# Sliding-window attention with ALiBi feeding an ELU feed-forward: bias by matmul for one more unit, and the first chunks' schedule rearranged

## The chip, the cores and the metric

The kernel runs on one core of a Trainium2 chip. The metric is the device time of one execution in microseconds; the number that counts is the median of several executions. A core has five engines with a queue each: TensorE (PE; its weight loads are listed apart as PEld), VectorE (DVE), ScalarE (ACT), GpSimd (POOL) and SyncE (SP). Each engine takes its instructions strictly in the order in which the program issues them, and waits for the other engines through semaphores.

## The reference

Two parts. Attention with 8 batches, 8 heads, 576 positions and 64 dimensions a head; a position sees itself and the 127 before it, with a linear distance penalty by head (ALiBi). Its output, 4608 tokens by 512, goes through a feed-forward of 2048 hidden units with ELU.

```python
scores = q @ k.T / sqrt(64) - slope[head] * |i - j|      # kept where 0 <= i - j < 128
attn = softmax(scores)
x = (attn @ v).reshape(4608, 512)
h = x @ w_in
g = where(h > 0, h, exp(min(h, 0)) - 1)
out = g @ w_out
```

## The kernel before

The work is cut into *steps*, numbered from 0. A step is a group of hidden matmuls (`hidden`, L279: 16 matmuls of 128 columns, or the same amount otherwise cut) into one of the PSUM banks of `BUF`, followed by its exponential on ScalarE (L284), its minimum with 1 on GpSimd (L285) and, one step later, the last part of the ELU on VectorE (`elu`, L292; `done(s)` issues the elus of step s). TensorE may write the next group into a bank only when the elu of the group before it there has run. A dictionary `HID` gives each step its group, `OUT` its four output matmuls of 512 columns (L298), and `at(s, f, ...)`, `before`, `after` hang further work on a step. All is written out by hand: the order of issue is the order of these lists. In steps 18 to 23 there is no hidden group.

The attention is cut by batch b and *unit* u, a block of 128 keys with the 256 queries that see it; the fourth unit (u = 3) is 192 queries of key block 3 and 64 of the last, half-filled block 4. A unit is scores (L172 for batches 0 and 1, L221 for the others), exponentials into the tile EX (L201, L206, L227), and values with the sums beside them (`values`, L244), divided on VectorE (L250, L251) into xn. xn is then turned into xT, the layout in which the hidden groups read it: by four TensorE transposes and a copy (`turn` with a copy, L263 and L264) for the first two batches, by a DMA transpose on SP (L259) for later ones.

The distance penalty enters in one of two ways. For units 0 to 2 of batch 0 it is added ahead of the scores in PSUM by a matmul of a scaled identity SI with the table RB (`bias`, L161; `early_bias`, L179). For all others the exponential is multiplied on VectorE by a table TAB of exponentials (`first_weigh`, L212, for batches 0 and 1; `weigh`, L232, for the others). TAB has two halves, the second for u = 3, copied on VectorE at the start (L367, L368).

q and k of batches 0 and 1 are turned by TensorE (`turn_first`, L133, with copies in L137). From batch 2 on, q and k lie in a staging tile st, and VectorE transposes them in blocks (`turn_qk`, L141): eight instructions a batch, four for k and four for q, each over all 576 positions. `TURN` lists the steps of these eight for batch 2; for later batches they come two by two, every fourth step. `START[b]` is the first step of batch b from batch 2 on.

Loads (`load_first`, `load_qk`, `load_v`, `load_wi`, `load_wo`) are issued from GpSimd's queue and stand there between the minimums of L285. Stores and DMA transposes stand in SP's queue.

The steps around the change, in batch 0: the scores of the third unit in step 3, those of the fourth unit in steps 4 and 6, its multiplications in steps 6 and 8, its values in step 9, the turn of the third tile in step 6:

```python
        at(6, first_scores, 0, 3, 1, 0)
        at(6, turn, 0, 2, nc.scalar.copy, sp[3])
        at(6, first_weigh, 0, 3, 0)
        at(7, first_expo, 0, 3, 1, 0, 0, 256)
        at(8, first_weigh, 0, 3, 1)
        at(9, values, 0, 3, 0)
```

Of the kernel before, what the change touches and what calls it, by code (L numbers as in the profile page):

```python
# [8 lines left out]
F16 = mybir.dt.float16  # L9
I32 = mybir.dt.int32  # L10
AF = mybir.ActivationFunctionType
ALU = mybir.AluOpType
# [6 lines left out]
def kernel(  # L19
# [9 lines left out]
    nc = tc.nc  # L29
# [7 lines left out]
    R = S // 64  # L37
    V = nc.vector
# [10 lines left out]
    def one(shape, dt, name):  # L49
        return const.tile(shape, dt, name=name, tag=name)  # L50

    ident = one([128, 128], F16, "ident")

    RB = one([128, 256], F16, "RB")

    SI = one([128, H, 128], F16, "SI")

    TAB = one([128, 2, 4, 2, 256], F16, "TAB")
# [15 lines left out]
    sp = [spa[:, 0, :], spa[:, 1, :]] + [ps_s.tile([128, 512], F32, name=f"sp{i}", tag=f"sp{i}") for i in (2, 3)]  # L74
# [4 lines left out]
    pairs = [AB, sp[2:4], hp, [sp[3], op]]  # L79
# [44 lines left out]
    def turn_first(b, w, part, half, bank, copy):  # L124

        p0, n, m, r0, j0 = split(b, w, part)
        nh = 4 if n == 32 or m == 1 else 2
        t = bank.bitcast(F16)[:, 0:nh * m * n].rearrange("p (x j r) -> p x j r", x=nh, j=m)
        r = slice(p0, p0 + n)
        for x in range(nh):  # L130
            for j in range(m):
                for hh in range(2):
                    nc.tensor.transpose(t[64 * hh:64 * hh + 64, x, j, :], s0[b][r, w, 4 * hh + nh * half + x, j0 + j, :],  # L133
                                        ident[r, r])
        t = t.rearrange("p x j r -> p x r j")
        o = (Q0, K0)[w][b][:, nh * half:nh * half + nh, r0:r0 + m * n]
        copy(o.rearrange("p x (r j) -> p x r j", j=m), t)  # L137
# [7 lines left out]
    with tc.manual_schedule():  # L145
# [8 lines left out]
        def blocks(u):  # L154
            return [(0, u, 128 * u, 256)] if u < 3 else [(0, 3, 384, 192), (192, 4, 512, 64)]

        def bias(half, d):
            for x in (2 * half, 2 * half + 1):
                for hh in range(2):
                    c = 256 * (x % 2)  # L160
                    nc.tensor.matmul(pairs[d][hh][:, c:c + 256], SI[:, 4 * hh + x, :], RB,  # L161
                                     start=x % 2 == 0, stop=False, skip_group_check=True)

        def first_scores(b, u, half, d):

            heads = [(x, hh) for x in (2 * half, 2 * half + 1) for hh in range(2)]
            added = b == 0 and u < 3
            for o, kb, q0, n in blocks(u):
                for x, hh in heads:
                    r, c = slice(64 * hh, 64 * hh + 64), 256 * (x % 2) + o  # L170
                    k0 = x * S + 128 * kb
                    nc.tensor.matmul(pairs[d][hh][:, c:c + n], kt_[b][r, k0:k0 + 128], Q0[b][r, x, q0:q0 + n],  # L172
                                     start=not added, stop=True, skip_group_check=True)

        def early_bias(banks, c0):

# [147 lines left out]
        rel = one([128, 256], I32, "rel")  # L324
        far = one([128, 256], F16, "far")
# [24 lines left out]
        V.tensor_scalar(out=ident, in0=rel[:, 0:128], scalar1=0.0, scalar2=None, op0=ALU.is_equal)  # L350
        V.scalar_tensor_tensor(out=far, in0=rel, scalar=127.0, in1=rel, op0=ALU.subtract, op1=ALU.mult)
        V.tensor_scalar(out=far, in0=far, scalar1=0.0, scalar2=-BIG, op0=ALU.is_gt, op1=ALU.mult)
        V.scalar_tensor_tensor(out=RB, in0=rel, scalar=-1.0, in1=far, op0=ALU.mult, op1=ALU.add)
        slope = [2.0 ** (-8.0 * (h + 1) / H) for h in range(H)]
        for h in range(H):
            V.tensor_scalar(out=SI[:, h, :], in0=ident, scalar1=8.0 * slope[h], scalar2=None, op0=ALU.mult)
        V.memset(VP[0][:, :, :, D:D + 1], 1.0)

        for h in range(H):
            nc.scalar.activation(TAB[:, 0, h // 2, h % 2, :], RB, AF.Exp, scale=slope[h])  # L360
        warm(22)
        turn_first(0, 1, 0, 0, hp[0], V.tensor_copy)
        turn_first(0, 1, 0, 1, op, V.tensor_copy)
        early_bias(AB, 0)
        turn_first(0, 0, 0, 0, hp[1], nc.scalar.copy)
        turn_first(0, 0, 0, 1, av, V.tensor_copy)
        V.tensor_copy(TAB[:, 1, :, :, 0:192], TAB[:, 0, :, :, 0:192])  # L367
        V.tensor_copy(TAB[:, 1, :, :, 192:256], TAB[:, 0, :, :, 0:64])  # L368
        early_bias(sp[2:4], 128)
# [59 lines left out]
        at(3, turn_first, 0, 1, 1, 1, sp[3], nc.scalar.copy)  # L429
        at(3, turn_first, 0, 0, 2, 0, hp[1], nc.scalar.copy)  # L430
        for half in range(2):
            at(3, bias, half, 3 * half)
        for half in range(2):
            at(3, first_scores, 0, 2, half, 3 * half)
            at(3, first_expo, 0, 2, half, 3 * half, 0, 256)
        at(4, first_scores, 0, 3, 0, 0)
        at(4, first_expo, 0, 3, 0, 0, 0, 256)
        at(5, values, 0, 2, 0)
        at(5, values, 0, 2, 1, op)
        at(6, first_scores, 0, 3, 1, 0)  # L440
        at(6, turn, 0, 2, nc.scalar.copy, sp[3])
        at(6, first_weigh, 0, 3, 0)
        at(7, first_expo, 0, 3, 1, 0, 0, 256)
        at(8, first_weigh, 0, 3, 1)
        at(9, values, 0, 3, 0)
        at(9, values, 0, 3, 1, sp[3])
        at(10, values, 0, 4, 0)
# [4 lines left out]

        for n in range(4):
            at(n + 1, load_wo, n)
        at(4, load_first, 1, 1, 0)
        at(5, load_first, 1, 0, 0)
        at(8, load_first, 1, 1, 1)
        at(10, load_first, 1, 0, 1)
        for n, s in enumerate((6, 7, 11, 12, 13)):
            at(s, load_v, 1, n)  # L460
        at(16, turn_first, 1, 1, 0, 0, av, V.tensor_copy)
        at(16, turn_first, 1, 1, 0, 1, sp[3], nc.scalar.copy)
# [14 lines left out]


        START = [None, None, 32, 49, 66, 83, 100, 117]
        TURN = 20, 22, 23, 24, 24, 25, 27, 29  # L480
        for b in range(2, B):
            for u in range(4):
                a = START[b] + 4 * u
                after(a, scores, b, u)
                for g in range(4):
                    before(a + 1 + g // 2, expo, b, u, g)
                at(a + 1, weigh, b, u, 0)
                at(a + 2, weigh, b, u, 1)
                at(a + 3, values, b, u, 0, sp[2])
                at(a + 3, values, b, u, 1, sp[3])  # L490
                at(a + 3, turn, b, u)
                if u == 3:
                    at(a + 4, values, b, 4, 0, sp[0])
                    at(a + 4, values, b, 4, 1, sp[2])
                    at(a + 4, turn, b, 4)
            a = START[b - 1] if b > 2 else 0
            for n in range(8):
                at(a + 4 * (n // 2) if a else TURN[n], turn_qk, b, int(n < 4), *divmod(n % 4, 2))
                at(a - 8 + n if a else 14 + n // 2, load_qk, b, int(n < 4), n % 4)
            for n in range(5):  # L500
                at(a + 3 + n if a else 18 + n // 2, load_v, b, n)

        slots = set(HID) | set(OUT) | set(tasks) | set(early)
        for s in range(min(slots), max(slots) + 1):
            for f, a in early.get(s, []):
                f(*a)
            for step in HID.get(s, []):
                hidden(*step)
            if s > 1 and s - 1 in HID:
                done(s - 1)  # L510
            for f, a in tasks.get(s, []):
                f(*a)
# [34 lines left out]
```

## Time and profile before

| what | value |
|---|---|
| median of 8 runs | 322.5 us (321.99 to 323.92) |
| the profiled execution by its own time | 322.0 us |
| its span, first to last instruction | 320.2 us |
| TensorE busy | 311.7 us, 97% |
| VectorE busy | 218.8 us, 68% |
| ScalarE busy | 181.1 us, 57% |
| GpSimd busy | 169.2 us, 53% |
| TensorE clock granted | full, in all slices of the page |

The profile is of one execution. Times in it are microseconds from the start of the span. A timeline row gives start, duration, engine, line and operation, the tiles written and read, the shape, the count of like instructions merged, and in brackets how long the engine was idle before it and what ended that. A waits row gives who waited for whom, total, number of times and the longest. Matmuls overlap their neighbours, and their ends are modelled; what TensorE takes is best read from one start to the next.

### The profile page before, as it was taken

Reading aid. Unit: us, or ns where it says so; the run is one execution under the profiler, and the core shown is the slowest. Engines: PE = TensorE matmul, PEld = TensorE weight load, DVE = VectorE, ACT = ScalarE, POOL = GpSimd, SP = SyncE. Lnnn points to the kernel's source line nnn. Section 1 sums busy time; section 2 is a strip of 40 time slices with the busy share of each in tenths; the row PEclk is TensorE's granted clock in tenths of the full one; section 3 lists DMA queues with packets and bytes.
Section 4 is the critical chain, followed back from the end, with each engine's and each line's share of the span. In section 5 each row is a group of like instructions: output and inputs, shape, how many; then the busy total and the mean of one; then the engine's idle time right before and its main releaser. Section 6 shows DMA issues by size and latency. Waiting matters only on the chain.

```text
span 320.2 us, 9418 instructions
## 1 busy us (share of the span) xinstructions
PE 311.7 (97%) x3967; PEld 220.2 (69%) x3967; DVE 218.8 (68%) x434; ACT 181.1 (57%) x322; POOL 169.2 (53%) x263
## 2 busy tenths in 40 slices
PE   8997999999999999999999999999999999999996
PEld 6786774677777777777666666666677666766653
DVE  4735747998777877777877777778777566653330
ACT  4577357576665465556666666646654655543431
POOL 8858787364656556663756365655633333333320
PEclk9999999999999999999999999999999999999999
DMA  9999999678799939795999778994911111120011
GB/s 102 198 193 206 198 179 170 76 81 93 84 92 125 132 53 117 96 120 86 100 99 123 109 85 93 123 133 65 111 51 51 43 50 52 51 57 35 33 61 72
DMA packets 95850, 32.00 MB, mean 100 GB/s; under 512 B 82880, under 2 KB 91328, under 8 KB 95808
## 3 DMA queue, kind: packets, MB, share of 16 engines
q0 software_dynamic: 75408, 18.36, 61.2%
q1 hardware_dynamic: 20400, 13.05, 16.3%
q8 instruction: 31, 0.51, 0.6%
q14 instruction: 11, 0.09, 0.1%
HBM read 36.70 MB, written 9.44 MB: 144 GB/s over the span
## 4 chain that ended last, share of the span: by engine, by line
PE 92%; DVE 4%; POOL 2%; issue 1%; ACT 1%; DVEq 0%; ACTq 0%
PE hp L279 36%; PE op L298 20%; PE av L298 16%; PE sp L244 4%; PE spa L221 4%; PE op L320 2%; PE sp L298 1%; PE sp L279 1%; POOL e L285 1%; DVE g L292 1%; PE av L312 1%; PE hp L133 1%; DVE EX L212 1%; DVE QT L141 1%; PE sp L133 1%
## 5 line engine op out<-in xcount | busy, mean ns | idle before, releaser
L285 POOL TENSOR_SCALAR e<-e 128x512 f32<-128x512 f32 x144 | 90.2, 627 | 138.7 <-ACT e L284 138.4
L279 PEld LDWEIGHTS <-wi 128*128 128x128 f16 x1856 | 124.5, 98 | 36.4 <-issue 6.3
L279 PE MATMUL hp<-xT,wi 128*128 128x128 f16 (+2 forms) x1728 | 143.9, 234 | 1.7 <-DVE g L292 1.7
L292 DVE SCALAR_TENSOR_TENSOR g<-e,hp 128x512 f16<-128x512 f32 x137 | 93.6, 684 | 54.8 <-POOL e L285 53.4
L284 ACT ACTIVATE e<-hp 128x512 f32<-128x512 f32 x137 | 82.1, 599 | 86.6 <-PE hp L279 82.5
L298 PE MATMUL op<-wo,g 128*128 128x512 f16 x304 | 77.5, 379 | 0.0
L298 PEld LDWEIGHTS <-g 128*128 128x128 f16 x560 | 50.1, 98 | 36.7 <-issue 1.1
L298 PE MATMUL av<-wo,g 128*128 128x512 f16 x240 | 61.4, 379 | 0.0
L232 DVE TENSOR_TENSOR EX<-EX,TAB 128x1024 f16<-128x1024 f16 x48 | 33.1, 690 | 15.3 <-ACT EX L227 15.3
L227 ACT ACTIVATE EX<-spa 128x512 f16<-128x512 f32 x48 | 26.1, 594 | 16.4 <-PE spa L221 16.4
L111 POOL DMA_DIRECT2D VP<-in_v_dram x40 | 35.0, 879 | 0.4 <-issue 0.3
L251 DVE TENSOR_TENSOR xn<-sp,rden 128x256 f16<-128x256 f32 (+1 forms) x60 | 25.4, 424 | 2.1
L227 ACT ACTIVATE EX<-sp 128x512 f16<-128x512 f32 x48 | 26.1, 600 | 0.0
L244 PEld LDWEIGHTS <-EX 128*128 128x128 f16 x576 | 22.2, 97 | 3.3 <-DVE EX L212 2.2
L244 PE MATMUL sp<-VP,EX 128*128 128x65 f16 x428 | 18.9, 193 | 0.9 <-DVE EX L212 0.8
L141 DVE STREAM_TRANSPOSE KT<-st 128x576 f16<-128x576 f16 x24 | 18.3, 803 | 0.0
L141 DVE STREAM_TRANSPOSE QT<-st 128x576 f16<-128x576 f16 x24 | 18.3, 803 | 0.0
L305 ACT COPY ob<-op 128x512 f32<-128x512 f32 x19 | 11.1, 586 | 9.7 <-PE op L298 9.4
L105 POOL DMA_DIRECT2D st<-in_k_dram x24 | 16.5, 687 | 0.1
L105 POOL DMA_DIRECT2D st<-in_q_dram x24 | 16.4, 684 | 0.0
L221 PEld LDWEIGHTS <-KT 32*128 32x128 f16 x480 | 8.9, 93 | 10.4 <-issue 10.2
L221 PE MATMUL spa<-QT,KT 32*128 32x256 f16 (+2 forms) x240 | 14.7, 248 | 0.0
(105 smaller groups left out, 192.0 us busy)
## 6 DMA issues: line engine op xcount, KB each, us to landing
out_dram<-ob SPq DMA_DIRECT2D x35, 256.0 KB, 2.2
VP<-in_v_dram POOLq DMA_DIRECT2D x32, 128.0 KB, 4.4
st<-in_k_dram POOLq DMA_DIRECT2D x24, 144.0 KB, 3.7
st<-in_q_dram POOLq DMA_DIRECT2D x24, 144.0 KB, 4.0
wi<-in_moe_w_in_dram POOLq DMA_DIRECT2D x4, 512.0 KB, 10.5
wo<-in_moe_w_out_dram POOLq DMA_DIRECT2D x4, 512.0 KB, 10.9
VP<-in_v_dram POOLq DMA_DIRECT2D x8, 64.0 KB, 4.3
s<-in_k_dram POOLq DMA_DIRECT2D x1, 512.0 KB, 12.1
```

The lines of the kernel that those rows point to most:

```text
L105: nc.gpsimd.dma_start(st[b][32 * g:32 * g + 32, w, :, :, :, :].rearrange("p h n j d -> p (h n) (j d)"), (q, k)[w][b, 2 * g:2 * g + 2, :, : ...
L111: nc.gpsimd.dma_start(VP[b % 2][0:p, n, :, 0:D], v[b, :, 128 * n:128 * n + p, :].rearrange("h p d -> p h d"))
L141: V.transpose(o, st[b][:, w, h2, n0:n1, :, 32 * dh:32 * dh + 32])
L221: nc.tensor.matmul(sp[g][:, 256 * h2 + o:256 * h2 + o + n], kt_[b % 2][r, k0:k0 + 128], QT[b % 2][r, h2, dh, q0:q0 + n], start=dh == 0, st ...
L227: nc.scalar.activation(unit(b, u)[:, g, :, :], sp[g].rearrange("p (h c) -> p h c", h=2), AF.Exp, scale=0.125)
L232: V.tensor_tensor(out=e, in0=e, in1=TAB[:, int(u == 3), 2 * gp:2 * gp + 2, :, :], op=ALU.mult)
L244: nc.tensor.matmul(a[:, x, h2, :], ex_[u][:, c:c + 128], VP[b % 2][:, n, 2 * g + h2, 0:D + 1], start=j == 0, stop=j == len(parts) - 1)
L279: nc.tensor.matmul(p[:, l * w + u0:l * w + u1], w_in_sb[:, c, fc * 128:(fc + 1) * 128], xT[:, c, x0:x0 + u1 - u0], start=(c == 0), stop=(c ...
L284: nc.scalar.activation(e[:, 0:n], p[:, 0:n], AF.Exp)
L285: nc.gpsimd.tensor_scalar(out=e[:, 0:n], in0=e[:, 0:n], scalar1=1.0, scalar2=0.0, op0=ALU.min, op1=ALU.max)
L292: V.scalar_tensor_tensor(out=gs[t][:, f0:f0 + nf, c0:c0 + w], in0=sh(es.pop((t, c0, f0))), scalar=1.0, in1=sh(hps.pop((t, c0, f0))), op0=A ...
L298: nc.tensor.matmul(o, gs[t][:, fc, ts * 128:(ts + 1) * 128], w_out_sb[:, fc, :], start=(fc == 0), stop=(fc == NFC - 1))
```

## The change

Five things are done:

- The fourth unit of batch 0 gets its distance penalty by matmul too. RB grows to 512 columns; its second half is filled by two VectorE copies at the start (192 and 64 columns of the first half: one for each of the fourth unit's two blocks). Eight matmuls of 256 columns are added, four ahead of each half of the unit's scores; the two multiplications of the unit fall away. TAB keeps both halves, for the later batches.
- Exponentials of the third and fourth unit are issued one step later, behind the exponential of a hidden group.
- The turn of the third tile goes from step 6 to step 7, its copy from ScalarE to VectorE; the second half of the fourth unit's scores goes from step 6 to step 7 as well. The elu of step 6 is issued behind them.
- Five loads of batch 1 (three of q and k, two of v) are issued one step later.
- The transposes of batch 2 are cut in two: the first 4 of 9 row blocks (k) or 6 of 9 (q) at the old steps, the rest in steps 32 to 38. The eight of batch 3 go from steps 32 to 44 to steps 40 to 48.

```diff
-    RB = one([128, 256], F16, "RB")
+    RB = one([128, 512], F16, "RB")
...
-        def bias(half, d):
+        def bias(u, half, d):
+            r0 = 256 * int(u == 3)
...
-                    nc.tensor.matmul(pairs[d][hh][:, c:c + 256], SI[:, 4 * hh + x, :], RB,
+                    nc.tensor.matmul(pairs[d][hh][:, c:c + 256], SI[:, 4 * hh + x, :], RB[:, r0:r0 + 256],
                                      start=x % 2 == 0, stop=False, skip_group_check=True)
...
-            added = b == 0 and u < 3
...
-                                     start=not added, stop=True, skip_group_check=True)
+                                     start=b > 0, stop=True, skip_group_check=True)
...
+        V.tensor_copy(RB[:, 256:448], RB[:, 0:192])
+        V.tensor_copy(RB[:, 448:512], RB[:, 0:64])
         V.tensor_copy(TAB[:, 1, :, :, 0:192], TAB[:, 0, :, :, 0:192])
...
-            at(3, bias, half, 3 * half)
+            at(3, bias, 2, half, 3 * half)
         for half in range(2):
             at(3, first_scores, 0, 2, half, 3 * half)
-            at(3, first_expo, 0, 2, half, 3 * half, 0, 256)
+            at(3 + half, first_expo, 0, 2, half, 3 * half, 0, 256)
+        at(4, bias, 3, 0, 0)
         at(4, first_scores, 0, 3, 0, 0)
-        at(4, first_expo, 0, 3, 0, 0, 0, 256)
+        at(5, first_expo, 0, 3, 0, 0, 0, 256)
         at(5, values, 0, 2, 0)
         at(5, values, 0, 2, 1, op)
-        at(6, first_scores, 0, 3, 1, 0)
-        at(6, turn, 0, 2, nc.scalar.copy, sp[3])
-        at(6, first_weigh, 0, 3, 0)
+        at(7, turn, 0, 2, V.tensor_copy, sp[3])
+        at(7, bias, 3, 1, 0)
+        at(7, first_scores, 0, 3, 1, 0)
         at(7, first_expo, 0, 3, 1, 0, 0, 256)
-        at(8, first_weigh, 0, 3, 1)
+        at(7, done, 6)
...
-        at(4, load_first, 1, 1, 0)
-        at(5, load_first, 1, 0, 0)
-        at(8, load_first, 1, 1, 1)
+        at(5, load_first, 1, 1, 0)
+        at(6, load_first, 1, 0, 0)
+        at(9, load_first, 1, 1, 1)
         at(10, load_first, 1, 0, 1)
-        for n, s in enumerate((6, 7, 11, 12, 13)):
+        for n, s in enumerate((7, 8, 11, 12, 13)):
             at(s, load_v, 1, n)
...
-        TURN = 20, 22, 23, 24, 24, 25, 27, 29
+        TURN = [None, None, (20, 22, 23, 24, 24, 25, 27, 29), (40, 40, 41, 42, 44, 44, 46, 48)]
+        REST = 32, 32, 36, 36, 33, 34, 37, 38
...
-                at(a + 4 * (n // 2) if a else TURN[n], turn_qk, b, int(n < 4), *divmod(n % 4, 2))
+                piece = (b, int(n < 4), *divmod(n % 4, 2))
+                if b == 2:
+                    m = 4 if n < 4 else 6
+                    at(TURN[b][n], turn_qk, *piece, 0, m)
+                    at(REST[n], turn_qk, *piece, m, R)
+                else:
+                    at(TURN[b][n] if b == 3 else a + 4 * (n // 2), turn_qk, *piece)
...
-            if s > 1 and s - 1 in HID:
+            if s - 1 in HID and s not in (1, 7):
                 done(s - 1)
```

More of the change, by code (lines that the diff above doesn't have):

```diff
@@ L352 @@
         V.tensor_scalar(out=far, in0=far, scalar1=0.0, scalar2=-BIG, op0=ALU.is_gt, op1=ALU.mult)
-        V.scalar_tensor_tensor(out=RB, in0=rel, scalar=-1.0, in1=far, op0=ALU.mult, op1=ALU.add)
+        V.scalar_tensor_tensor(out=RB[:, 0:256], in0=rel, scalar=-1.0, in1=far, op0=ALU.mult, op1=ALU.add)
         slope = [2.0 ** (-8.0 * (h + 1) / H) for h in range(H)]
@@ L359 @@
         for h in range(H):
-            nc.scalar.activation(TAB[:, 0, h // 2, h % 2, :], RB, AF.Exp, scale=slope[h])
+            nc.scalar.activation(TAB[:, 0, h // 2, h % 2, :], RB[:, 0:256], AF.Exp, scale=slope[h])
         warm(22)
```

## The prediction

> **What bounds the kernel now.** I read the busy times first, then the chain that ended last, the waits of TensorE between 20 and 80 us, the busy time by stretch, and the timeline of the stretches that are not full.
>
> ```profile
> PE 311.7 (97%) x3967; PEld 220.2 (69%) x3967; DVE 218.8 (68%) x434; ACT 181.1 (57%) x322; POOL 169.2 (53%) x263
> ...
> PE 92%; DVE 4%; POOL 2%; issue 1%; ACT 1%; DVEq 0%; ACTq 0%
> ```
> TensorE sets the end: what it is spared shortens the kernel one for one, and so does what it is given to do. Elsewhere only work that TensorE waits for counts.
>
> ```profile
> PE hp L279 <- DVE g L292: 1.7, 4, 0.7
> PE sp L244 <- DVE EX L212: 0.8, 1, 0.8
> PE sp L263 <- DVE xn L251: 0.6, 2, 0.3
> ```
> All its waits in that window are for VectorE, and they lie in two places. By stretch (columns: length, then PE, PEld, DVE, ACT, POOL busy):
>
> ```profile
> 22.20:33.20 11.00, 8.80 (x155) 7.56 (x152) 5.39 (x11) 7.64 (x12) 8.33 (x11) 1.00 1.38 200
> 33.20:49.00 15.80, 15.80 (x274) 12.46 (x272) 9.36 (x19) 8.12 (x13) 13.06 (x21) 1.00 1.83 186
> 58.00:76.00 18.00, 17.04 (x287) 13.38 (x285) 16.71 (x33) 10.52 (x17) 10.26 (x17) 1.00 0.72 93
> 91.00:109.60 18.60, 18.60 (x280) 13.70 (x278) 14.60 (x30) 10.49 (x19) 11.08 (x18) 1.00 1.13 110
> ```
> In the first, VectorE is half idle and GpSimd nearly full; in the third VectorE itself is full (16.71 of 18.00). In the second and fourth TensorE has no gap. The timeline of the gaps:
>
> ```profile
> 26.10 0.89 POOL L98 DMA_DIRECT2D s<-in_k_dram  x1
> 26.69 0.23 PE L263 MATMUL sp<-ident,xn 128*128 128x128 f16 x1 [0.31 <-DVE xn L251]
> 27.23 0.34 PE L263 MATMUL sp<-ident,xn 128*128 128x128 f16 x3 [0.32 <-DVE xn L251]
> 30.21 1.05 PE L279 MATMUL hp<-xT,wi 128*128 128x128 f16 x16 [0.72 <-DVE g L292]
> 32.35 0.41 PE L244 MATMUL sp<-VP,EX 128*128 128x65 f16 x8 [0.85 <-DVE EX L212]
> ...
> 61.87 0.65 DVE L292 SCALAR_TENSOR_TENSOR g<-e,hp 128x512 f16<-128x512 f32 x1
> 62.56 1.05 PE L279 MATMUL hp<-xT,wi 128*128 128x128 f16 x16 [0.27 <-DVE g L292]
> 64.85 1.05 PE L279 MATMUL hp<-xT,wi 128*128 128x128 f16 x16 [0.54 <-DVE g L292]
> 71.93 1.05 PE L279 MATMUL hp<-xT,wi 128*128 128x128 f16 x16 [0.16 <-DVE g L292]
> ```
> The bracket counts from the modelled end of the last matmul, about 0.16 us after its columns are in (16 of 128 columns show 1.05, but 0.89 where the next group follows at once). From start to start the gaps are 0.16 longer: 0.47 and 0.48 at the turn of the third tile, 0.88 before step 9, 1.01 before the fourth unit's values: 2.84 us in the first place. In the second: 0.43, 0.70, 0.32, and some 0.3 in three short ones at 53 to 64 us: 1.7 us.
>
> **First place: steps 3 to 10.** *Added:* eight ALiBi matmuls of 256 columns. The same ones for the third unit (L161) start 0.107 apart (21.20, 21.31, 21.41, 21.52), so 8 x 0.108 = +0.86 us of TensorE, nothing beside it to hide it. The weight loads run ahead, as L161's do.
> *Removed:* two VectorE multiplications (L212, 0.69 each at 28.28 and 31.61). The second ended at 32.30 and its values started at 32.35: that wait (1.01) goes, since the values then wait only for the exponential.
> *Moved:* I carry the queues on from 22.27 with durations from the rows (hidden group 0.89, exponential of 1024 columns 0.92 from start to start and 1.02 to its end, of 512 columns 0.60, minimum on GpSimd 0.61, elu 0.69, about 0.05 from one engine to the next).
> ScalarE now takes step 4's exponential (23.4 to 24.0) ahead of the third unit's second half, and step 5's (25.2 to 25.8) ahead of the fourth unit's first half; before, they ran at 24.04 and 25.42. GpSimd therefore has step 5's minimum at 25.9 and step 6's at 27.4, with the k and q loads (0.9 each to issue) now behind each and not ahead: before, 27.01 and 28.52, the latter stretched to 0.91. VectorE: elu of step 5 at 26.55, the third tile's copy at 27.7 to 28.1 (a new VectorE row, 0.43, taken off ScalarE; it waits for the turn until 27.65, with elu 6 and 7 queued behind it), elu of step 6 at 28.05 to 28.75.
> TensorE: step 4 at 22.27, bias and scores to 24.0, step 5 at 24.1, values 24.99 to 25.5, step 6 at 25.5, step 7 at 26.4, the turn at 27.3 (its xn is ready at 26.65: no wait), bias and scores to 28.3, step 8 at 28.4 (its xT at 28.1: 0.26 spare), step 9 at 29.3 (its elu at 28.75: 0.5 spare), values 30.2 to 30.65, first output group at 30.7. Before, that group started at 32.61. Next in line is the turn of the fourth tile: its xn (behind elu 8, itself behind a v load on GpSimd) comes at 32.8, 0.14 late. Step 12 then starts at 35.1 where it was 36.87. Sum: 2.84 + 0.1 - 0.86 - 0.2 to 0.3 = **-1.8 us**.
> The moved loads: k needs 12.1 us to land and is issued 0.35 later, at 26.45, so 38.6; it is turned at 44.39 - 1.8 = 42.6. q at 27.9 + 13.3 = 41.2, wanted at 45.5. The two v loads and the second k piece go one step later and are wanted after 50. Past 35 us GpSimd shows gaps again (1.15 at 35.24). SP holds nothing ahead of its first store at 42.42, so the turn passes none of its rows. So the loads cost nothing.
>
> **Second place: steps 20 to 31.** The eight transposes of batch 2 (0.816 alone; 0.72 from start to start, as 60.47 to 61.19) shrink to 4/9 and 6/9 of their rows there. [...] I take 0.12: pieces of 0.39 and 0.52, the rests 0.45 and 0.32. Split, the eight cost 6.7 instead of 5.8 us[...]; but it is paid in steps 32 to 38, and steps 20 to 29 lose 4 x 0.33 + 4 x 0.20 = 2.1 us of VectorE.
> Elu 24 (its minimum was ready at 60.8, it ran at 61.87) comes at 61.0, and step 26 follows step 25 and the output without a wait (-0.43). Elu 25 then starts when GpSimd delivers, near 62.8, which is when the scores end: -0.70. Elu 29 leaves the transpose at 70.50 behind sooner: -0.32. With the short ones, and 0.2 for minimums that are late in turn: **-1.5 us** (ends: 0 if a piece costs what a whole one does, -1.74 if all go).
>
> **Steps 32 to 49.** VectorE idles 0.5 ahead of most elus, and TensorE's step comes 0.4 to 1.5 after the elu it needs (elu at 95.08 to 95.77, its step at 96.17). In steps 32 to 38 rests of 3.1 us replace 2.9 us of whole ones. In 40 to 48 eight whole ones stand where four did: +2.9 us into 18.60 - 14.60 = 4.0 free. Each goes behind a multiplication, where 0.5 is idle: 94.46 + 0.72 pushes elu 41 from 95.08 to 95.2, within 0.4. The last, in step 48, ends near 109.8, ahead of the scores of batch 3 at 110.7. I take 0 (ends 0 and +0.9, three pushes of 0.3). The first two score groups of batch 2 read only rows of the first pieces, and in the changed program's order they wait for none of the rests.
>
> **Start.** Two small copies into RB stand in VectorE's queue ahead of the TAB copies (8.84 to 10.10); 0.61 is idle ahead of the next row at 10.71. [...] The row: the TAB copy of 512 columns took 0.70, that of 1536 columns 0.64, while GpSimd issued a 0.96 load. By size the pair costs 0.3 to 0.4 (hidden), at 0.70 each 1.4 - 0.6 = +0.8. I take 0: [...] GpSimd's load is over at 9.98.
>
> **Sum.** -1.8 - 1.5 + 0 + 0 = -3.3 us. The profiled run took 322.0 us by its own time, with a span of 320.2; the median is 322.5. So span 316.9, profiled run 318.7, median **319.2 us**. After 76 us every stage is full of TensorE work, so what is won stays.
>
> **Rivals.**
> *Half of it (chance 0.23).* In the first place GpSimd was busy 8.33 of 11.00; if its minimums stay the bound, the waits of elu 6 to 9 come back one step later and only 0.8 of 1.8 stays; or the pieces cost what whole transposes do, and the second place gives nothing. For it: minimums stretched to 0.91 near VectorE's multiplications. Against: two of these go away, and the loads now stand behind the minimums. Time: 322.5 - 1.8 or - 2.3, about 320.5.
> *Start held (0.06).* [...] 319.2 + 0.8 = 320.0.
> *Slower (0.07).* VectorE's queue in steps 33 to 48 becomes the bound: the sixteen transposes there stand ahead of elus, and every one that takes more than the 0.9 of room (0.5 idle, 0.4 slack) holds the next hidden step. A multiplication that met GpSimd took 1.07 at 62.44. The point is a mean hold of 3.3 / 16 = 0.2 us; at 0.3, 322.5 - 3.3 + 4.8 = 324.0. Against: half of the sixteen are pieces of 0.3 to 0.45, and no transpose row is above 0.84.
>
> **Numbers.** Full gain 0.64 (own range 318.5 to 320.1), half 0.23, start 0.06, slower 0.07. This kernel's measurement tells about 0.3%, 1.0 us, from no change. Faster by more than that: 0.90, within 0.03, slower 0.07. The range 318.4 to 320.9 leaves out the slower case and the ends beyond half.
>
> **What would show it.** Right: no gap before the fourth unit's values, the first output group near 30.7, step 12 near 35.1, elu 24 and 25 ending ahead of their hidden steps, eight L163 rows more of 0.27, transpose rows near 0.48 and 0.6, and no TensorE wait from 76 to 110 us. Wrong: "PE hp <- DVE g" still at 1.5 us or more, a new wait of TensorE on xT at step 8, transposes of 0.8 for pieces, or elus of steps 41 to 48 late.

## The result, and the profile after

The changed kernel takes 319.89 us (median of 11 runs, 318.7 to 321.79) where the kernel before, beside it, takes 322.51: ratio 0.9917, interval 0.9902 to 0.9932. Run again later beside three variants, it took 319.2 us (318.6 to 319.73) where the kernel before took 322.24: ratio 0.9895, interval 0.9866 to 0.9924. So it gains 2.6 to 3.0 us where 3.3 was forecast.

The profiled execution of the changed kernel took 320.99 us, with a span of 319.2. That is only 1.0 less than before, because of its start, which comes last in this section. Line numbers are those of the changed kernel, one higher than before at most places (L293 is the elu; `bias` is L163, the copies into RB are L368 and L369).

From the page, the busy times and the chain that ended last:

```profile
PE 312.3 (98%) x3975; PEld 221.4 (69%) x3975; DVE 218.6 (68%) x443; ACT 180.9 (57%) x321; POOL 169.2 (53%) x263
...
PE 92%; DVE 2%; POOL 2%; DMA 2%; issue 1%; ACT 0%; POOLq 0%; ACTq 0%
```

TensorE has eight matmuls more; VectorE's share of the chain has gone from 4% to 2%. What TensorE waited for between 20 and 80 us is a single line, where there were four: the three for VectorE, and `PE hp L133 <- issue: 0.3, 1, 0.3`, which the prediction left out when it said that all were for VectorE. Waits whose bracket is under 0.15 are in no such list.

```profile
PE hp L134 <- issue: 0.5, 1, 0.5
```

By stretch (length, then PE, PEld, DVE, ACT and POOL busy with their counts, granted clock, DMA share, GB/s):

```profile
24.20:33.20 9.00, 9.00 (x163) 8.07 (x160) 4.23 (x10) 7.41 (x11) 6.52 (x10) 1.00 1.29 205
33.20:49.00 15.80, 15.65 (x273) 12.39 (x271) 9.28 (x19) 7.89 (x13) 13.87 (x21) 1.00 1.85 179
58.00:76.00 18.00, 17.91 (x313) 14.26 (x311) 15.41 (x35) 10.86 (x18) 10.99 (x17) 1.00 0.84 101
91.00:109.60 18.60, 18.60 (x277) 13.67 (x276) 16.35 (x33) 10.49 (x19) 10.80 (x18) 1.00 0.95 110
```

In the first place TensorE has no idle time left up to 33.20; in the stretch behind it, which was full before, 0.15 of idle time has come up. In the second place VectorE has 1.3 us of slack more (15.41 of 18.00 where it was 16.71). In the stretch to which its work went (91.00 to 109.60) VectorE is 1.75 fuller, and TensorE still has no gap.

The timeline of the first place. Times here are 2.03 us later than in the profile of before, as the whole execution is; take that off to compare them with the forecast:

```profile
29.30 0.39 PE L264 MATMUL sp<-ident,xn 128*128 128x128 f16 x4
...
29.72 0.42 DVE L265 COPY xT<-sp 128x512 f16<-128x512 f16 x1 [0.46 <-PE sp L264]
...
30.11 0.69 DVE L293 SCALAR_TENSOR_TENSOR g<-e,hp 128x512 f16<-128x512 f32 x1
...
30.38 1.96 PE L280 MATMUL hp<-xT,wi 128*128 128x128 f16 x32
...
32.18 0.41 PE L245 MATMUL av<-VP,EX 128*128 128x65 f16 x8
...
32.67 1.02 PE L299 MATMUL op<-wo,g 128*128 128x512 f16 x4
...
34.50 0.42 DVE L252 TENSOR_TENSOR xn<-sp,rden 128x256 f16<-128x256 f32 x1
...
34.97 0.38 PE L264 MATMUL sp<-ident,xn 128*128 128x128 f16 x4
```

The third tile's turn, its copy, the elu of step 6, steps 8 and 9 in one piece (x32), the fourth unit's values and the first output group follow each other as forecast: 27.27, 27.69, 28.08, 28.35, 30.15 and 30.64 on the clock of before, where 27.3, 27.7, 28.05, 28.4, 30.2 and 30.7 were written. One wait is left: the fourth tile's turn at 34.97 stands 0.31 behind the end of the values, for an xn that ended at 34.92.

To see the gains apart from the start, I cut every profile at four landmarks on ScalarE: the third unit's first exponential, and the exponentials of steps 12, 32 and 50. All in us:

| kernel | start | to step 12 | 12 to 32 | 32 to 50 | median | ratio to before, 95% |
|---|---|---|---|---|---|---|
| before | 22.16 | 15.80 | 37.28 | 37.09 | 322.51 | |
| after | 24.19 | 14.11 | 35.93 | 37.09 | 319.89 | 0.9902 to 0.9932 |
| e11_after_again | 21.84 | 14.09 | 35.92 | 37.09 | 319.20 | 0.9866 to 0.9924 |
| e1_first_only | 22.11 | 14.11 | 37.28 | 37.09 | 320.79 | 0.9923 to 0.9958 |
| e2_second_only | 22.76 | 15.80 | 35.94 | 37.09 | 321.19 | 0.9942 to 0.9982 |
| e3_rb_later | 22.70 | 14.11 | 36.34 | 37.09 | 319.90 | 0.9881 to 0.9946 |
| e4_no_bias | 22.85 | 14.36 | 36.36 | 37.09 | 320.29 | 0.9893 to 0.9953 |
| e5_bias_only | 22.47 | 15.19 | 37.28 | 37.09 | 321.61 | 0.9963 to 0.9984 |
| e6_loads_only | 21.72 | 15.25 | 37.28 | 37.09 | 321.73 | 0.9968 to 0.9987 |
| e7_split_in_place | 22.58 | 15.78 | 37.39 | 37.09 | 322.37 | 0.9983 to 1.0001 |
| e8_double_b3 | 21.58 | 14.09 | 35.97 | 40.61 | 323.10 | 1.0009 to 1.0037 |
| e9_elu8_later | 22.16 | 13.93 | 36.02 | 37.09 | 318.82 | 0.9860 to 0.9917 |
| e10_loads_spread | 22.43 | 14.10 | 35.93 | 37.09 | 319.20 | 0.9867 to 0.9927 |
| e12_both | 22.68 | 13.92 | 35.92 | 37.09 | 318.79 | 0.9863 to 0.9939 |

The first place gained 15.80 - 14.11 = 1.69, the second 37.28 - 35.93 = 1.35, steps 32 to 50 nothing: 3.04 in all. The rest behind step 50 is 207.9 in both. The start of this one execution was 2.03 later, and 2.03 - 3.04 is the 1.01 by which its span is shorter.

That late start, in the timeline of the changed kernel:

```profile
8.37 0.44 PE L134 MATMUL hp<-ident,s 64*64 64x64 f16 x16 [1.34 <-DMA s<-in_q_dram]
...
9.72 0.65 DVE L368 COPY RB<-RB 128x192 f16<-128x192 f16 x1
9.84 0.56 DVE L369 COPY RB<-RB 128x64 f16<-128x64 f16 x1
9.92 0.87 DVE L370 COPY TAB<-TAB 128x1536 f16<-128x1536 f16 x1
...
12.75 0.18 DVE L251 RECIPROCAL rden<-hp 128x4 f32<-128x4 f32 x1 [1.34 <-PE hp L245]
```

The first q load was issued at 2.48 in both kernels and landed at 8.32 here, at 6.89 before. TensorE waited 1.34 us for it, and after that the granted clock was 0.65 and then 0.78: TensorE took up the turn of q 0.87 later (8.37, before 7.50), and needed 1.16 more from there to the landmark (15.82, before 14.66). By stretch:

```profile
8.00:11.00 3.00, 2.63 (x57) 2.19 (x58) 1.89 (x5) 0.96 (x2) 2.59 (x4) 0.65 1.50 183
11.00:14.00 3.00, 2.61 (x32) 1.81 (x31) 1.53 (x5) 2.60 (x5) 2.83 (x11) 0.78 1.37 201
```

Such a drop is not the change's own: five of the 80 executions of the kernel before that were timed beside the experiments have a mean granted clock of 0.995 or less (323.16 to 325.21 us), and here two of the eleven (320.99 and 321.79), without which the median would be 319.74.

The two copies into RB have long rows (0.65 and 0.56), but start 0.12 and 0.08 before what follows them. The copy of TAB behind them takes 0.80 to the start of the next where it took 0.56, and VectorE then sits idle for 1.34 before its next reciprocal. So this profile does not show that they held anything; the experiments below take that up.

### The profile page after: what moved, and what is told of

Read it like the earlier page. It is cut to its first block, busy times and chain, and to the rows that moved or that the text cites. A ratio compares the mean times of both kernels' runs of the same rounds, so it can differ in the third digit from the quotient of the medians.

```text
span 319.2 us, 9444 instructions
## 1 busy us (share of the span) xinstructions
PE 312.3 (98%) x3975; PEld 221.4 (69%) x3975; DVE 218.6 (68%) x443; ACT 180.9 (57%) x321; POOL 169.2 (53%) x263
## 4 chain that ended last, share of the span: by engine, by line
PE 92%; DVE 2%; POOL 2%; DMA 2%; issue 1%; ACT 0%; POOLq 0%; ACTq 0%
PE hp L280 37%; PE op L299 20%; PE av L299 16%; PE spa L222 4%; PE sp L245 4%; DMA s<-in_q_dram 2%; PE sp L280 1%; PE sp L299 1%; POOL e L286 1%; POOL s L99 1%; PE av L313 1%; DVE xn L252 1%; PE spa L173 1%; PE sp L134 1%; DVE g L293 1%
## 5 line engine op out<-in xcount | busy, mean ns | idle before, releaser
L293 DVE SCALAR_TENSOR_TENSOR g<-e,hp 128x512 f16<-128x512 f32 x137 | 93.5, 682 | 53.4 <-POOL e L286 52.4
L142 DVE STREAM_TRANSPOSE QT<-st 128x576 f16<-128x576 f16 (+2 forms) x28 | 19.1, 714 | 0.0
L142 DVE STREAM_TRANSPOSE KT<-st 128x576 f16<-128x576 f16 (+2 forms) x28 | 18.8, 710 | 0.0
L222 PE MATMUL sp<-QT,KT 32*128 32x256 f16 (+2 forms) x240 | 14.7, 248 | 0.0
```

What stands on the lines that cost most here:

```text
L142: V.transpose(o, st[b][:, w, h2, n0:n1, :, 32 * dh:32 * dh + 32])
L222: nc.tensor.matmul(sp[g][:, 256 * h2 + o:256 * h2 + o + n], kt_[b % 2][r, k0:k0 + 128], QT[b % 2][r, h2, dh, q0:q0 + n], start=dh == 0, st ...
L293: V.scalar_tensor_tensor(out=gs[t][:, f0:f0 + nf, c0:c0 + w], in0=sh(es.pop((t, c0, f0))), scalar=1.0, in1=sh(hps.pop((t, c0, f0))), op0=A ...
```

## The experiments

My theory was that the two places are independent, that each gives what its queues allow, and that nothing else in the change counts. Its rivals: the RB copies hold the start; part of the gain comes back as another wait; the split, the matmuls or the moved loads carry a place alone.

### Each place alone

One kernel has the first place's edits and the old transposes, the other the new transposes and nothing else.

```diff
 # e1_first_only, against after
-        TURN = [None, None, (20, 22, 23, 24, 24, 25, 27, 29), (40, 40, 41, 42, 44, 44, 46, 48)]
-        REST = 32, 32, 36, 36, 33, 34, 37, 38
+        TURN = 20, 22, 23, 24, 24, 25, 27, 29
 ...
+                at(a + 4 * (n // 2) if a else TURN[n], turn_qk, b, int(n < 4), *divmod(n % 4, 2))
```

e2_second_only makes the opposite edit in the kernel before.

> Steps 3 to 10 as in the changed kernel, the transposes of batches 2 and 3 whole and at their old steps. Theory (the two places add up): from the third unit's first exponential to step 12's exponential 14.1 us as in the changed kernel (15.8 before), from step 12 to step 32 the old 37.3; time 1.7 below before, 0.995 of it. Rival (the transposes were hiding what the first place wins): with TensorE arriving 1.7 earlier at a VectorE queue that is as full as it was, the second stretch grows to 38 or more, and less than 1 us is left.

> Steps 3 to 10 as before; batch 2's transposes in two pieces, batch 3's at steps 40 to 48. Theory: step 12 to step 32 35.9 us (37.3 before), first stretch the old 15.8, steps 32 to 50 the old 37.1; time 1.3 below before. Rival (the split's fixed cost and the fuller steps 40 to 48 eat it): steps 32 to 50 grow by 0.5 or more, time within 0.5 of before.

They add to the whole. To step 12 e1 has all of it (14.11) and e2 nothing (15.80); from step 12 to 32 it is the other way round (37.28 and 35.94). The medians, 1.77 and 1.37 under the 322.56 that the kernel before took beside them, sum to 3.1. The wait lines of TensorE from 20 to 80 us that each leaves, besides one `issue` line of 0.4 and 0.5, e1 first:

```profile
PE hp L280 <- DVE g L293: 1.0, 3, 0.5
```

```profile
PE sp L244 <- DVE EX L212: 0.8, 1, 0.8
PE hp L279 <- DVE g L292: 0.7, 1, 0.7
PE sp L263 <- DVE xn L251: 0.6, 2, 0.3
```

Each keeps the waits of the place that it leaves alone, and has none of the other's. What is not taken apart is the second place: no run puts the rests in steps 32 to 38 and leaves batch 3's transposes at their old steps.

### Do the copies into RB hold the start?

e3_rb_later issues them in step 2, behind the TAB copies and the first units' work.

```diff
-        V.tensor_copy(RB[:, 256:448], RB[:, 0:192])
-        V.tensor_copy(RB[:, 448:512], RB[:, 0:64])
 ...
+        def fill():
+            V.tensor_copy(RB[:, 256:448], RB[:, 0:192])
+            V.tensor_copy(RB[:, 448:512], RB[:, 0:64])
+
+        at(2, fill)
```

> The changed kernel with the two RB copies issued in step 2, out of the start. Theory (the start's spread is the landing of the first loads, and the copies are hidden): time as the changed kernel, 319.9 within 0.4, and the idle of VectorE ahead of the first reciprocal grows by what the copies took, 0.2 to 0.4. Rival (the copies hold the start): 0.4 to 0.8 below the changed kernel, so 319.1 to 319.5.

The median is that of the changed kernel, 319.90 beside 319.89. The start landmark goes with the landing of the first q load instead. It is 21.58 to 21.84 where that landed at 6.72 to 6.81 (e8, e6, e11), 22.11 to 22.47 for 6.89 to 7.48, 22.58 to 22.85 for 7.68 to 8.16, and 24.19 for 8.32, with the copies at their place (after, e1, e5, e8 to e12) as without them (before, e2, e4, e6, e7). In the second profile of the changed kernel the load landed at 6.72 and the start was at 21.84, the clock full in every slice. The medians alone could not settle it, since the interval of this run is 2.1 us wide; the landmark against the landing does. So the copies cost nothing that these runs can tell, and the 24.19 came of a late load and a low clock in one execution. They do take room: with the load at 7.68 to 7.83, VectorE idles 0.76 ahead of its first reciprocal in the kernels without them (e2, e3, e7) and 0.10 in e12 with them. Why this load lands up to 1.6 us apart is open.

This run showed something else: steps 12 to 32 took 36.34, not 35.93. From its timeline:

```profile
42.17 0.70 POOL L106 DMA_DIRECT2D st<-in_k_dram  x1 [1.08 <-DMA s<-in_q_dram]
43.34 0.66 POOL L106 DMA_DIRECT2D st<-in_k_dram  x1 [0.48 <-DMA VP<-in_v_dram]
...
44.02 0.63 POOL L286 TENSOR_SCALAR e<-e 128x512 f32<-128x512 f32 x1
...
44.68 0.69 DVE L293 SCALAR_TENSOR_TENSOR g<-e,hp 128x512 f16<-128x512 f32 x1 [2.88 <-POOL e L286]
45.29 1.22 DVE L138 COPY KT<-av 128x1024 f16<-128x1024 f16 x1
...
46.56 0.64 PE L134 MATMUL av<-ident,s 128*64 128x128 f16 x16 [0.34 <-DMA st<-in_k_dram]
```

GpSimd's issues of batch 2's k stood still for 1.08 and 0.48 us, each until a load of batch 1 had landed. That is the eighth issue before: in all 14 profiles the loads of this queue use eight semaphores by turns, and none was issued less than 0.28 us after the landing of the load eight issues earlier, which had the same semaphore (that least one is in the changed kernel; in the kernel before the least is 0.98). The minimum at 44.02 stood behind them, the elu at 44.68 behind it, the copy of KT behind that; and TensorE's turn of q, which writes the bank that this copy reads, started 0.05 after its end. The bracket's DMA is merely the last semaphore of several: for the cause one goes by the rows. TensorE lost 0.41 there (36.34 - 35.93).

### What the eight matmuls buy, and what the order buys

Three kernels take the first place apart. e4_no_bias is the changed kernel with the multiplications of the fourth unit back, in steps 7 and 8, and no copies into RB. e5_bias_only is the kernel before with the matmuls for those multiplications and nothing moved. e6_loads_only is the kernel before with the five loads one step later, and no other edit.

```diff
 # e4_no_bias, against after
-        at(4, bias, 3, 0, 0)
-        at(7, bias, 3, 1, 0)
+        at(7, first_weigh, 0, 3, 0)
+        at(8, first_weigh, 0, 3, 1)
 # e5_bias_only, against before (with RB, its copies and bias as in after)
+        at(4, bias, 3, 0, 0)
+        at(6, bias, 3, 1, 0)
-        at(6, first_weigh, 0, 3, 0)
-        at(8, first_weigh, 0, 3, 1)
 # e6_loads_only, against before
-        at(4, load_first, 1, 1, 0)
-        at(5, load_first, 1, 0, 0)
-        at(8, load_first, 1, 1, 1)
+        at(5, load_first, 1, 1, 0)
+        at(6, load_first, 1, 0, 0)
+        at(9, load_first, 1, 1, 1)
-        for n, s in enumerate((6, 7, 11, 12, 13)):
+        for n, s in enumerate((7, 8, 11, 12, 13)):
```

> The changed kernel, but the fourth unit of batch 0 is multiplied on VectorE as before (in steps 7 and 8), without the eight bias matmuls and the RB copies; order, loads and the turn as in the changed kernel. Theory (the matmuls buy the values' wait): TensorE is spared 0.86, but waits some 0.8 to 1.3 for the second multiplication behind elu 7; first stretch 14.3 to 14.7 (14.1 changed, 15.8 before), time 0.2 to 0.6 above the changed kernel. Rival (order alone wins, the matmuls are a loss): first stretch 13.3, time 0.8 below the changed kernel.

> The kernel before with one thing changed: the fourth unit of batch 0 has its bias by matmul (steps 4 and 6) and no multiplication. Theory (TensorE's waits are queues on GpSimd and VectorE, so what is added to TensorE there fills waits): the wait of 1.01 for the values goes, the 0.86 of matmuls lies in the waits for elu 6 (0.88) and elu 4, first stretch 14.7 to 15.1 (15.8 before), time 0.7 to 1.1 below before. Rival (added TensorE work counts in full): 15.8 - 1.01 + 0.86 = 15.65.

> The kernel before with one thing changed: the five loads of batch 1 one step later. Theory (step 9 waited for GpSimd's queue, where two loads stood ahead of minimums): the 0.88 ahead of step 9 goes and the second multiplication moves up with elu 7, first stretch 14.8 to 15.1 (15.8 before). Rival (the wait moves to the values whole): 15.6 or more.

To step 12 they took 14.36, 15.19 and 15.25: e4 as expected, e5 and e6 0.09 and 0.15 above their ranges, though well below their rivals. What TensorE still waited for in e4:

```profile
28.61 1.95 PE L279 MATMUL hp<-xT,wi 128*128 128x128 f16 x32 [0.18 <-DVE xT L264]
...
31.60 0.41 PE L244 MATMUL sp<-VP,EX 128*128 128x65 f16 x8 [0.80 <-DVE EX L212]
```

in e5:

```profile
30.21 1.05 PE L280 MATMUL hp<-xT,wi 128*128 128x128 f16 x16 [0.43 <-DVE g L293]
...
33.79 0.40 PE L245 MATMUL av<-VP,EX 128*128 128x65 f16 x8 [0.28 <-DVE xn L252]
```

and in e6 (besides the two waits of the third tile's turn, which stay at 0.30 and 0.32):

```profile
29.16 1.05 PE L279 MATMUL hp<-xT,wi 128*128 128x128 f16 x16 [0.25 <-DVE g L292]
...
31.36 0.41 PE L244 MATMUL sp<-VP,EX 128*128 128x65 f16 x8 [0.90 <-DVE EX L212]
```

So no single edit gives the first place. (Sums from here to the end of this section are from start to start, each stretch against the same one before.)

In e5 both halves of the matmuls stand ahead of the third tile's turn, which before waited twice for a division, and they fall into that wait: from step 4 to step 7 TensorE takes 5.20 where it took 5.14. The wait for the multiplication goes (1.02), and the one at step 9 is 0.37 shorter. But 0.71 comes back at the fourth tile: 0.45 ahead of the values at 33.79, and 0.27 at the turn behind them. That leaves the gain of 0.61.

The loads alone gain 0.55, all of it at step 9 (bracket 0.72 before, 0.25 here), since GpSimd's minimum then stands ahead of a load and not behind it.

Apart they give 0.61 + 0.55; with the exponentials and the turn moved, all give 1.69. Without the matmuls e4 has 1.44 of that. So on top of the order they are worth 14.36 - 14.11 = 0.25. Three waits of e4 went: 0.97 ahead of the values, 0.25 ahead of step 8, and 0.25 ahead of the third unit's second values (for an exponential that ended at 25.64). For them came 0.92 of added work (0.49 for the first four matmuls, 0.43 for the others), and 0.27 at the fourth tile's turn. No run moves the exponentials or the turn alone.

### What a piece of a transpose costs

e7_split_in_place is the kernel before with batch 2's transposes in two pieces, both at the old step.

```diff
+                if b == 2:
+                    m = 4 if n < 4 else 6
+                    at(TURN[n], turn_qk, *piece, 0, m)
+                    at(TURN[n], turn_qk, *piece, m, R)
```

> The kernel before, batch 2's eight transposes each cut in two pieces that stand one behind the other at the old steps. It prices the fixed cost of an instruction where VectorE is the bound. Theory: 0.10 from start to start for each of eight more instructions, two or three of them ahead of each elu that TensorE waits for; step 12 to step 32 grows from 37.3 to 37.6 to 37.9. [...]

Steps 12 to 32 grew by 0.11, less than the 0.3 to 0.6 expected. So the split by itself gains nothing; what e2 gains comes from where the rests stand. In its timeline, two pairs and the elu behind them:

```profile
60.90 0.85 DVE L141 STREAM_TRANSPOSE KT<-st 128x256 f16<-128x256 f16 x2
61.65 0.81 DVE L141 STREAM_TRANSPOSE QT<-st 128x384 f16<-128x384 f16 x2
62.37 0.65 DVE L292 SCALAR_TENSOR_TENSOR g<-e,hp 128x512 f16<-128x512 f32 x1
```

A pair takes 0.75 and 0.72 from start to start; whole ones took 0.72 and 0.68 (60.47, 61.19, 61.87 before). One instruction more costs 0.03 to 0.04 us, where I had estimated 0.12. The pieces of these two pairs take 0.36 (256 columns), 0.39 (320), 0.47 (384) and 0.25 (192) from start to start: they go nearly by columns, 1.2 to 1.4 ns each.

### How full is VectorE in steps 40 to 48?

e8_double_b3 issues each of the eight transposes of batch 3 twice: 8 x 0.72 = 5.8 us more of VectorE in the stretch where the slower rival would decide.

```diff
-                    at(TURN[b][n] if b == 3 else a + 4 * (n // 2), turn_qk, *piece)
+                    for _ in range(2 if b == 3 else 1):
+                        at(TURN[b][n] if b == 3 else a + 4 * (n // 2), turn_qk, *piece)
```

> The changed kernel with each of batch 3's eight transposes in steps 40 to 48 done twice. It finds the point of the rival in which VectorE becomes the bound there. Theory (about 0.9 us of room are left in these steps, 18.6 - 14.6 - 2.9 - the rest's idle): 5.8 us more are 4.9 too many, steps 32 to 50 grow from 37.1 to 40.5 or up to 42. If instead the room is much larger, as the rows without any TensorE wait in these steps would allow, they grow by less than 2.

From step 32 to 50 it took 40.61, 3.52 more, and it is slower than the kernel before (323.10, interval 1.0009 to 1.0037). TensorE's wait line from 75 to 115 us:

```profile
PE hp L280 <- DVE g L293: 2.8, 5, 1.0
```

In the changed kernel TensorE waits for nothing there. So the slower rival had the right place and the right mechanism, and lacked the size: the 2.9 us that came into these steps went into free time, and of the next 5.8 us only 2.2 did.

### Can the rest be had?

The changed kernel has two leftovers: the 0.31 at the fourth tile's turn, and the loads that wait for a landing.

```diff
 # e9_elu8_later, and e12_both
+        at(9, done, 8)
 ...
-            if s - 1 in HID and s not in (1, 7):
+            if s - 1 in HID and s not in (1, 7, 9):
 # e10_loads_spread, and e12_both
-        for n, s in enumerate((7, 8, 11, 12, 13)):
+        for n, s in enumerate((7, 8, 18, 18, 19)):
             at(s, load_v, 1, n)
```

> The changed kernel with one line of order more: the elu of step 8 is issued on VectorE behind the divisions of the fourth unit's values, so that the fourth tile's xn no longer stands behind it. Theory: the 0.31 us wait of TensorE at the turn of the fourth tile (34.97 in the changed kernel's profile) is VectorE's order, as the third tile's was; with the divisions ahead it goes, and the elu, about 1.0 us later, is still in time for step 10: the stretch from the third unit's first exponential to step 12 is 13.8 us where the changed kernel has 14.11, and the median 0.3 below the changed kernel's in the same call. Rival: the elu then comes late for its step, and what is won at the turn is lost one step on: 14.1 or more.

> The changed kernel with three loads of batch 1's v (the third to fifth) issued in steps 18, 18 and 19 where it has them in steps 11, 12 and 13. Theory: the 0.4 to 0.5 us wait near 46.5 us that two of the variants showed (step 17's turn of q, behind the elu of step 15, behind a minimum that stands on GpSimd behind a load which cannot be issued before an earlier one has landed) and half a us of idle time on GpSimd before the first loads of batch 2's k come from too many loads at once; with three fewer in front GpSimd issues batch 2's k without waiting for a landing, the stretch of steps 12 to 32 stays at 35.9 us, and the median is 0.2 to 0.4 below the changed kernel's in the same call. Rival: the loads were no cause of the missing 0.4 us, and the median is the same within 0.15; or the v loads then come late for batch 1's third unit, which would show as a wait for a transfer near 56 to 64 us and a stretch above 36.3.

> The changed kernel with both edits, the elu of step 8 behind the fourth unit's divisions and the three loads of v in steps 18 to 19. Theory: the two gains lie in different stretches and add: to step 12 13.8 us, steps 12 to 32 35.9 us, median 0.5 to 0.7 below the changed kernel's in the same call. Rival: what TensorE gains ahead of step 12 it waits for later, since transfers land at their own time: the first stretch 13.8, the second 36.2 or more, and the median that of the changed kernel.

> The changed kernel once more, on the same chip as the three others, for a second profile and a time to compare them with. If its late start in the first profile (24.19 us to the third unit's first exponential) was chance and not the copies into RB, the start lies between 21.6 and 23 here as in the other kernels; if it belongs to the kernel, near 24 again. The stretch to step 12 is 14.1 us in both cases; steps 12 to 32 are 35.9 us, or 36.3 if the wait near 46.5 us falls into this execution.

e9 gained 0.17 to step 12, not 0.3. From its timeline:

```profile
32.63 0.39 PE L264 MATMUL sp<-ident,xn 128*128 128x128 f16 x4
...
33.42 0.42 DVE L252 TENSOR_TENSOR xn<-av,rden 64x256 f16<-64x256 f32 x1
...
33.89 0.40 PE L245 MATMUL av<-VP,EX 128*128 128x65 f16 x8
```

The turn now waits for nothing, but the next values wait 0.14 for a division that reads their bank and that stands behind the same elu. In e10 the issues of batch 2's k follow each other at once:

```profile
40.90 1.35 POOL L106 DMA_DIRECT2D st<-in_k_dram  x2
```

With three loads fewer in front, no issue waited for a landing. But the median did not move: 319.20 (318.95 to 319.45), the changed kernel beside it 319.20. Its own profiles have 35.93 and 35.92 from step 12 to 32, so this wait was not in them. It was in three of the seven profiles that have the first place's gain and the loads where the changed kernel has them: by the table 0.41 us in e3, 0.43 in e4, 0.09 in e9. That is 0.13 on average, which six executions cannot show. e12 has both edits and 318.79; the 0.4 that it and e9 lie below the changed kernel is within their intervals, and I claim no better version.

## Why the prediction was right, and by how much its terms were off

The forecast was 319.2 us with a range of 318.4 to 320.9; the two measurements are 319.89 and 319.20, and the case was the likeliest one, the full gain.

**First place, -1.8: -1.69.** The queues, carried on row by row from 22.27, hold to 0.06 us down to the first output group. The minimums of GpSimd there take 0.60 to 0.63, and none is stretched to 0.91 beside a multiplication: that was the case against "half of it", and it held. Two terms of the sum were off by less than 0.1 each: the first gap at the third tile's turn, behind scores, was 0.38 and not 0.47, and the eight matmuls took 0.92 and not 0.86. What was mis-sized most is the wait next in line, the fourth tile's turn: 0.14 was forecast, 0.31 measured, because xn came at 32.89 on the old clock (32.8 forecast) and TensorE a little earlier than written. "Next in line is the turn of the fourth tile" was right, its size was half. e9 shows that VectorE's order caused it.

**Second place, -1.5: -1.35.** The timeline around elu 24 and 25, with the start of their hidden steps:

```profile
60.61 0.47 DVE L142 STREAM_TRANSPOSE KT<-st 128x256 f16<-128x256 f16 x1
60.97 0.56 DVE L142 STREAM_TRANSPOSE QT<-st 128x384 f16<-128x384 f16 x1
...
61.44 0.65 DVE L293 SCALAR_TENSOR_TENSOR g<-e,hp 128x512 f16<-128x512 f32 x1
...
62.28 1.06 PE L280 MATMUL hp<-xT,wi 128*128 128x128 f16 x16
...
63.20 0.69 DVE L293 SCALAR_TENSOR_TENSOR g<-e,hp 128x512 f16<-128x512 f32 x1
...
63.94 1.05 PE L280 MATMUL hp<-xT,wi 128*128 128x128 f16 x16
```

On the old clock (take off 2.03 - 1.69 = 0.34) the elus run at 61.10 and 62.86, forecast 61.0 and 62.8. Step 26 follows without a wait, so its 0.43 went as written. Step 27 still waits 0.10, and 0.51 went, where 0.70 was written. Of that 0.70, 0.09 was never there: the 0.16 that the prediction adds to each bracket holds behind hidden groups and values, but behind scores it is 0.07 (the next group starts 0.33 after their start, their row is 0.40). For the rest, elu 25 starts "when GpSimd delivers", as forecast, but its minimum took 0.67 and not 0.61 (62.50 to 63.17, beside a multiplication). "Elu 29 leaves the transpose sooner: -0.32" failed by most of its size: 0.22 of that wait is still there. The rows from elu 28 to step 30, those of the changed kernel first, then those of before:

```profile
68.38 0.69 DVE L293 SCALAR_TENSOR_TENSOR g<-e,hp 128x512 f16<-128x512 f32 x1 [0.45 <-POOL e L286]
...
69.34 0.80 POOL L286 TENSOR_SCALAR e<-e 128x512 f32<-128x512 f32 x1 [0.36 <-ACT e L285]
69.59 0.61 DVE L142 STREAM_TRANSPOSE QT<-st 128x384 f16<-128x384 f16 x1
...
70.17 0.69 DVE L293 SCALAR_TENSOR_TENSOR g<-e,hp 128x512 f16<-128x512 f32 x1
...
70.92 1.05 PE L280 MATMUL hp<-xT,wi 128*128 128x128 f16 x16
```

```profile
69.30 0.69 DVE L292 SCALAR_TENSOR_TENSOR g<-e,hp 128x512 f16<-128x512 f32 x1 [0.45 <-POOL e L285]
...
70.50 0.83 DVE L141 STREAM_TRANSPOSE QT<-st 128x576 f16<-128x576 f16 x1
71.23 0.65 DVE L292 SCALAR_TENSOR_TENSOR g<-e,hp 128x512 f16<-128x512 f32 x1
```

From its start to that of elu 29 the piece took 0.58 (69.59 to 70.17) where the whole one took 0.73 (70.50 to 71.23). It saved 0.15, and not the 0.20 of the prediction's own price, let alone 0.32: the minimum of elu 29, beside a multiplication too, took 0.80 and ended at 70.14, 0.03 ahead of it. The elu then took 0.69 for 0.65, so that about 0.1 was left. Taking 0.2 off for late minimums was the right kind of term; with the short waits at 0.3, as written, 0.3 would have been its size.

**The price of a piece.** The 0.12 that I took was my estimate of a fixed part in each instruction; no row had shown it. Measured in place, one instruction more costs 0.03 to 0.04 (e7). The sizes say the same: from 0.25 for 192 columns to 0.72 for 576 it is 1.22 ns a column, which leaves 0.02. Little hung on it, since the rests are paid where VectorE has room.

**Steps 32 to 49, 0: 0.** Measured 37.09 in both kernels. The eight whole transposes in steps 40 to 48 take 0.77 to 0.83 by their rows, and no elu came late for TensorE. e8 puts the limit between the 5.8 us that are there and twice that.

**Start, 0: 0.** The rival of the held start fell: the rows of the copies are long, but what they took was hidden. In seven of the eight profiles with the copies at their place a row of theirs is longer than 0.20, and it ends within 0.04 of the end of a load's issue on GpSimd (both at 10.37 in the changed kernel, both at 9.97 in e12). Why they end together these runs do not show. But two long rows do not add up: in the changed kernel the copies start 0.12 apart and end 0.03 apart. And the reciprocal behind them still starts on TensorE's signal; the room left was 0.10 in e12 and 0.34 or more in the others.

**"So the loads cost nothing".** The median of e10 shows no gain from fewer loads, but the reasons given were incomplete. I asked when each load would land and who wants it. I did not ask what is queued behind a load that cannot be issued yet: in three of seven profiles that cost 0.09 to 0.43 us near 46 us.

**What stays open.** The two measurements of the changed kernel, 2.6 and 3.0 under the kernel before, overlap in their intervals, and the landmarks give 3.04. Whether late starts or the wait near 46 us made the first one smaller can't be told from times alone.

## What to carry to other kernels

Where one engine sets the end and each of its waits is for another engine's queue, carrying the queues on row by row gives each wait within some 0.2 us (0.14 was forecast for 0.31, none for 0.10 and 0.22); the errors lie in what comes next in line, so take something off for each wait that can come up in place of the one removed. An edit that removes a wait by adding nearly the same time of work on the bound engine (0.92 for 1.02 here) gains only where the added work falls into another wait, and part comes back: 0.61 alone, 0.25 on top of the new order. The order of the queues and the loads gave 1.44 of the 1.69. When TensorE is moved forward in time, look at what does not move with it: in e3, with TensorE 1.69 us ahead, GpSimd's queue stood for 1.08 and 0.48 us until loads had landed, and TensorE lost 0.41 by what stood behind them.

## What the runs showed of the hardware that was not expected

- The loads behind which GpSimd stood still point to the program and not to the chip: a load waits for the one eight issues earlier, whose semaphore it uses (in the changed kernel five were issued 0.28 to 0.29 us after that one's landing). The first k of batch 2 waited from 0.39 (after) to 1.19 us (e4) for it; with three loads fewer in front of it it did not wait at all (e10).
- Small VectorE instructions in a row cost little beyond their columns: 0.36 and 0.39 us from start to start for two pieces of 256 and 320 columns, 0.72 for one of 576. A row's own duration (0.47 for 256 columns) overlaps the next by about 0.1.
- A minimum on GpSimd (128x512, float32) that no VectorE multiplication in SBUF overlaps took 0.63 us at most in the profiles of before and after; every longer one overlapped one, up to 0.80 in the changed kernel (69.34) and 0.91 in the kernel before (28.52, 31.86). Once, at 62.35 before, the minimum kept its 0.61 and the multiplication took 1.07.
- The first q load, issued at 2.48 us each time, landed between 6.72 and 8.32. After the longest wait for it (1.34 us) the granted clock was 0.65 and 0.78 for the next two stretches of 3 us, and matmuls of 128 columns started 0.107 apart where the same ones start 0.057 apart in the profile of before; in half microseconds it was 0.91 from 8.5, 0.50 from 9.0 to 12.0 and 0.67 up to 12.5, so half of full for about 3.4 us. After a wait of 1.24 us (e7) it stayed full (1.00 from 4.0 to 14.0); why one wait had this effect and the other had not is open.
